# Seven half-size products in the first matmul of an attention and MLP kernel, with the LayerNorm gain folded into its weights

## Chip, cores and metric

The kernel runs on one core of a Trainium2 chip. The metric is the device time of one execution in microseconds, taken as the median of several. The kernel before took 280.4 us (median of 8 runs, 279.99 to 280.83).

## What is computed

Eight batches of 576 positions go through a linear attention with 8 heads of 64 columns, and the result x (512 columns) through LayerNorm and a two-layer MLP, with x added at the end.

```python
q_s = softmax(q over head_dim); k_s = softmax(k over positions)   # attention
kv  = einsum('bhsd,bhse->bhde', k_s, v)
x   = einsum('bhsd,bhde->bhse', q_s, kv)      # then heads side by side: 576 x 512 a batch
xn  = (x - mean) / sqrt(var + 1e-6) * g_ln
ch  = maximum(xn @ w_ch1, 0.0) @ w_ch2        # 512 -> 2048 -> 512
out = x + ch
```

## The kernel before

**Chunks.** The rows are cut into nine chunks of 512. Chunk c = 0 to 7 holds positions 0 to 511 of batch c, as 4 row groups `t` of 128; chunk 8 (`C9`) holds the last 64 positions of all eight batches. The code counts from 0 throughout, and so does this text.

**First matmul (MLP).** `xn` is transposed to `xnT`, so that its 512 columns are 4 blocks `ko` of 128 partitions. The 2048 hidden columns are 16 row tiles `m` of the transposed hidden state `hT`. `mm1` makes one row tile from 4 matmuls of 512 columns (one for each `ko`, all four row groups); `mm1_part` makes it for two row groups, with 256 columns. In chunks 2 to 8 row tiles 0 to 3 are made by `mm1_part`, 4 to 15 by `mm1`. `relu` moves each result from PSUM to `hT` on ACT (DVE takes some of chunk 0). The factor 1/std is left out of `xn` and applied at the end (`rstd_op`, `y_quarter`), since the relu commutes with a positive factor per row.

**Second matmul.** From chunk 1 on (`FAST`) it is already in Strassen's form: `mm2_fast` makes seven products of half-size blocks, 16 matmuls of 256 columns each, from `hT`, its four sums `hs` (`sum_h`, DVE) and four sums of w2 made once (`quarter_w2`). The PSUM banks are called a, b, c, e (in chunk 8 also d). Several results share products, so a bank is copied in the middle (`seed_c`, `copy_u("s2")`, `copy_u("s3")`, on ACT), products go on adding to it, and a copy is added to another bank on DVE (`seed_e`, `add_u`). Chunk 8 has its own order, `last_products`: products 1, 2, 6, 5, 7, 3, 4.

**Attention of the next chunks, as side work.** While PE works on the MLP of chunk c, the kernel also does the attention of chunk c + 1 (`attn_fast`: q reductions, `kv_mm`, evacuation to `kv_sb`, `po_mm`, `x_fast`, `xn_T`) and prepares batch c + 2 (`prep_fast`: exp of q and k on ACT, the transpose `eq_T`, the cast of v to `vm`, the remainders by `prep_kvrem`). `x_fast` scales the attention result by 1/sum of q, with the row sum as a by-product, makes the mean and calls `xn_out`, which subtracts the mean and multiplies with the broadcast gain `g_bc`. `square_sum` makes the variance on ACT.

**What sets the order.** The order on each engine is written out by hand. `run(main, side)` walks the matmuls of the chunk, each with a weight (1 for 512 columns, 0.5 for 256), and issues each piece of side work when the sum of weights reaches its number (its due time). A chunk of 512 rows has 64 + 56 = 120 units. A due time only sets the place in each engine's queue; the engines run ahead of or behind each other as their semaphores let them.

**Transfers.** SP's queue issues the loads of q, k, v and their remainders from batch 3 on, and the transposes. POOL's queue issues the weights, batches 1 and 2, and the stores of the output. v is loaded as float32 to `vt` and cast to bf16 in `vm` by ACT (batches 3 to 7), or cast by the transfer to a bf16 `vt` and copied by DVE (`CAST`: batches 1 and 2).

**PSUM.** `mm_ps` has 6 banks for the MLP, `att_ps` 2 for the attention.

Of the kernel before, what the change touches and what calls it, by code (L numbers as in the profile page):

```python
# [3 lines left out]

# [16 lines left out]
def kernel(  # L21
# [33 lines left out]
    CAST = (1, 2)  # L55
    T0 = 6
# [13 lines left out]

    ident = const.tile([P, P], BF16)
    eps_ln = const.tile([P, 1], FP32)
# [6 lines left out]
    g_bc = const.tile([P, DM], FP32)  # L79
# [22 lines left out]
    raws = {}  # L102

# [3 lines left out]
    def alloc_kv(b):  # L107
        raws[b][0], raws[b][1], raws[b][3], raws[b][4] = (
            raw.tile([P, H, T, D], FP32, tag="kt", name="kt", bufs=1),
            raw.tile([P, H, T, D], BF16 if b in CAST else FP32, tag="vt", name="vt", bufs=1),  # L110
            raw.tile([P, H // 2, D], FP32, tag="ktr", name="ktr"),
            raw.tile([P, H // 2, D], FP32, tag="vtr", name="vtr"),
        )
# [47 lines left out]
    def prep_kvrem(b):  # L161
        par = b % 2
        nc.scalar.activation(ekr[:, par], raws[b][3], AF.Exp)
        for half in range(2):
            ps = slice(SR * half, SR * half + SR)
            nc.vector.tensor_copy(
# [52 lines left out]
    def exp_k0(j):  # L219
        hs = slice(2 * j, 2 * j + 2)  # L220
        if j == 0:
            eks[0] = raw.tile([P, T0, H, D], BF16, tag="vt", name="ek0", bufs=1)
# [8 lines left out]
    def z0_mm(j):  # L231

        if j % 2 == 0:
            kvbox["z0", j // 2] = mm_ps.tile([P, 2, 256], FP32, tag="m", name="z0")
# [38 lines left out]
    def start_x(c):  # L273
# [3 lines left out]
            mlp.tile([P, T, DM], BF16, tag="xn", name="xn"),  # L277
# [6 lines left out]
    def po_mm(c, t, i):  # L284


        if c < B:
            if i == 0:
                pool, tag = (mm_ps, "m") if c == 0 and t >= 2 else (att_ps, "a")
                pobox["p"] = pobox[c, t] = pool.tile([P, DM], FP32, tag=tag, name="po")  # L290
# [22 lines left out]
    def stats(c, t, src, parts=(slice(0, 512),)):  # L313
# [3 lines left out]
        for cols in parts:  # L317
            nc.vector.scalar_tensor_tensor(
                xn[:, t, cols], in0=src[:, cols], scalar=mv[:, t, 0:1], in1=g_bc[:, cols],
# [3 lines left out]
    def square_sum(c, t):  # L323
        x, _, _, mv = xs[c]
# [4 lines left out]
    def xn_out(c, t):  # L329
        x, _, xn, mv = xs[c]  # L330
        nc.vector.scalar_tensor_tensor(  # L331
            xn[:, t], in0=x[:, t], scalar=mv[:, t, 0:1], in1=g_bc, op0=ALU.add, op1=ALU.mult
        )

    def x_fast(c, t):
# [7 lines left out]
        )  # L343
        nc.vector.tensor_scalar_mul(out=mv[:, t, 0:1], in0=st[:, t, 0:1], scalar1=-1.0 / DM)
# [15 lines left out]
    def xn_sub(c, t):  # L360
        _, _, xn, mv = xs[c]
        nc.vector.scalar_tensor_tensor(
            xn[:, t], in0=pobox[c, t], scalar=mv[:, t, 0:1], in1=g_bc, op0=ALU.add, op1=ALU.mult
# [25 lines left out]
    def rstd_op(c):  # L389
# [4 lines left out]
            lnv, mv[:, :, 1], AF.Ln, bias=eps_ln, scale=1.0 / DM  # L394
        )
        nc.scalar.activation(rstds[c], lnv, AF.Exp, scale=-0.5)
# [12 lines left out]
    def mm1(c, m, ko):  # L409
        if m == 0 and ko == 0:  # L410
            new_h()
        if ko == 0:
            hbox["ph"] = mm_ps.tile([P, T, P], FP32, tag="m", name="ph")
# [7 lines left out]
    def mm1_part(c, m, t0, tn, ko):  # L421

        if (m, t0, ko) == (0, 0, 0):
            new_h()
        half, at = divmod(t0, 2)
        if m % 2 == 0 and at == 0 and ko == 0:
            hbox["ph", m // 2] = mm_ps.tile([P, 2, 2, P], FP32, tag="m", name="ph")
# [4 lines left out]
            start=(ko == 0), stop=(ko == KO1 - 1),  # L432
# [27 lines left out]
    def mm2(c, t, ko):  # L460
        if ko == 0:
            hbox["pc"] = mm_ps.tile([P, DM], FP32, tag="m", name="pc")
# [7 lines left out]
    def mm2_stream(c, t, ko):  # L470

        if ko == 0:
            hbox["pc", t] = mm_ps.tile([P, DM], FP32, tag="m", name="pc")
# [7 lines left out]
    def quarter_w2(i, g):  # L481
# [6 lines left out]
        nc.vector.tensor_sub(out=dst, in0=x, in1=y)  # L488

# [34 lines left out]
    def bank(name):  # L524
        hbox[name] = mm_ps.tile([P, 2, DH2], FP32, tag="m", name="b" + name)
# [25 lines left out]
    def last_products(product):  # L551
# [28 lines left out]
        def seed_e():  # L580
            bank("e")
            add_u("e", "s2")

        product(1, "a", first=True, at={
            0: [lambda: sum_h(1, 0), lambda: sum_h(1, 1)],
            15: [lambda: both("a", 0, 0), lambda: sum_h(1, 2), lambda: sum_h(1, 3)]})
        product(2, "c", first=True, at={15: [lambda: both("c", 0, 0, True), lambda: store(0, 2, 0)]})
        product(6, "a", at={15: [lambda: copy_u("s2")]})
        product(5, "b", first=True)
        product(7, "a", at={1: [seed_e, lambda: both("b", 2, 1)], 15: [  # L590
# [7 lines left out]
    def mm2_fast(c):  # L598
# [33 lines left out]
        def sums(*which):  # L632
            return [lambda g=g, i=i: sum_h(g, i) for g, i in which if g or c == FAST]

        late = c == FAST
# [12 lines left out]
    def mlp_steps(c):  # L648
        full = range(KO2)
# [412 lines left out]
```

## Time and profile before

| what | value |
|---|---|
| median of 8 runs | 280.4 us |
| the profiled execution: its own time, its span | 280.14 us, 278.4 us |
| busy share of PE, DVE, ACT, POOL | 98%, 70%, 65%, 13% |
| granted clock of TensorE | 0.998 |
| chunks 2 to 6, starting at 79.74 us | 28.11, 28.10, 28.11, 28.11, 28.10 us |
| chunk 8 with the end | 30.09 us |
| first matmul, 512 columns (L414) | 368 matmuls |
| first matmul, 256 columns (L429) | 400 matmuls, 32 more of 128 columns |
| second matmul, 256 columns (L521) | 896 matmuls |

The page lists busy time by engine. A matmul's own duration is its latency, and matmuls overlap, so that the rate of a stream is read from the time of a run of them and not from the mean of one. Idle time of an engine that isn't the bound costs nothing. A bracket behind a row of the timeline gives the idle time before it and what ended it.

### The profile page before, as it was taken

To read this page: it belongs to the slowest core of one execution; us is meant where nothing else is said; L and a number is where in the kernel's file an instruction comes from. 1 tells how busy PE (TensorE), PEld (TensorE's weight loads), DVE (VectorE), ACT (ScalarE), POOL (GpSimd) and SP (SyncE) were. 2 spreads that over 40 slices of the span, in tenths; PEclk is the share of its full clock that TensorE was granted. 3 is DMA by queue.
4 is the path that set the end of the run, shared out by engine and by line. 5 is a ranking of instruction groups with operands and counts; after the bars stand their busy time and mean duration, and the time that the engine had idled before them with its cause. 6 is when DMAs were issued, how large, how long until landed. Compare 5 with 4: busy or idle time off the path is not lost.

```text
span 278.4 us, 5663 instructions
## 1 busy us (share of the span) xinstructions
PE 271.9 (98%) x2242; PEld 201.4 (72%) x2245; DVE 195.4 (70%) x457; ACT 181.8 (65%) x346; POOL 36.8 (13%) x64
## 2 busy tenths in 40 slices
PE   8999999999999999999999999999999999999994
PEld 6688855766995699558955995589659855885683
DVE  4672647988996688658865886588657929962363
ACT  4568862797887785778567866886585477526500
POOL 3832224300030003000300030003000300030000
PEclk9999999999999999999999999999999999999999
DMA  7999999899979996994599469545914410241014
GB/s 189 248 206 208 337 218 334 192 248 314 186 161 364 280 142 171 325 223 79 145 338 235 77 155 316 100 75 129 212 38 79 134 57 1 40 128 61 2 38 113
DMA packets 68844, 48.01 MB, mean 172 GB/s; under 512 B 40401, under 2 KB 65489, under 8 KB 68818
## 3 DMA queue, kind: packets, MB, share of 16 engines
q1 hardware_dynamic: 57074, 27.66, 42.7%
q0 software_dynamic: 11152, 19.47, 27.8%
q10 hardware_dynamic: 592, 0.52, 0.6%
q8 instruction: 17, 0.28, 0.4%
q14 instruction: 9, 0.07, 0.1%
HBM read 36.70 MB, written 9.44 MB: 166 GB/s over the span
## 4 chain that ended last, share of the span: by engine, by line
PE 90%; DMA 4%; DVE 3%; issue 0%; POOL 0%; DVEq 0%
PE ph L414 29%; PE ba L521 20%; PE ph L429 15%; PE bb L521 5%; PE be L521 5%; PE bc L521 5%; PE pc L474 4%; PE pkv L259 3%; DMA v<-in_v_dram 2%; PE po L291 2%; DMA qt<-in_q_dram 2%; DVE x L338 1%; PE ptr L803 1%; DVE xn L331 1%; PE po L298 1%; DVE kv_sb L268 0%
## 5 line engine op out<-in xcount | busy, mean ns | idle before, releaser
L414 PE MATMUL ph<-xnT,w_sb 128*128 128x512 bf16 x368 | 87.2, 379 | 0.0
L402 ACT ACTIVATE hT<-ph 128x512 bf16<-128x512 f32 x92 | 53.5, 598 | 18.4 <-PE ph L414 18.4
L414 PEld LDWEIGHTS <-w_sb 128*128 128x128 bf16 x368 | 34.0, 98 | 34.5 <-issue 0.2
L521 PEld LDWEIGHTS <-hs 128*128 128x128 bf16 x512 | 49.2, 98 | 5.7 <-DVE hs L505 0.2
L429 PE MATMUL ph<-xnT,w_sb 128*128 128x256 bf16 (+1 forms) x432 | 52.7, 269 | 0.0
L439 ACT ACTIVATE hT<-ph 128x512 bf16<-128x512 f32 x48 | 28.6, 600 | 24.5 <-PE ph L429 24.3
L505 DVE TENSOR_TENSOR hs<-hT 128x1024 bf16<-128x1024 bf16 x32 | 21.9, 688 | 27.8 <-ACT hT L402 27.6
L429 PEld LDWEIGHTS <-w_sb 128*128 128x128 bf16 x432 | 38.4, 98 | 4.0 <-DMA w_sb<-in_moe_w_ch_dram 0.2
L521 PEld LDWEIGHTS <-hT 128*128 128x128 bf16 x384 | 36.6, 98 | 5.2 <-ACT hT L402 0.2
L538 POOL DMA_DIRECT2D out_dram<-ot x28 | 15.0, 540 | 179.7 <-DVE ot L532 155.9
L521 PE MATMUL ba<-w_q,hs 128*128 128x256 bf16 x256 | 31.3, 273 | 0.0
L331 DVE SCALAR_TENSOR_TENSOR xn<-x,mv,g_bc 128x512 bf16<-128x512 bf16 x34 | 25.6, 752 | 1.2
L338 DVE SCALAR_TENSOR_TENSOR x<-po,rq 128x512 bf16<-128x512 f32 x30 | 20.6, 686 | 6.5 <-PE po L291 6.1
L325 ACT ACTIVATE scrap<-x,mv 128x512 bf16<-128x512 bf16 x34 | 24.6, 723 | 0.1
L291 PE MATMUL po<-kv_sb,eqT 128*128 128x128 bf16 x128 | 24.1, 219 | 0.4 <-DVE x L338 0.2
L199 DVE TENSOR_REDUCE zq<-eq 128x8 f32<-128x512 bf16 x32 | 20.1, 687 | 4.2 <-ACT eq L191 2.4
L259 PE MATMUL pkv<-vm,ek 128*128 128x129 bf16 x112 | 21.2, 220 | 0.0
L546 ACT COPY s<-ba 128x512 f32<-128x512 f32 x15 | 8.8, 585 | 16.7 <-PE ba L521 16.7
L291 PEld LDWEIGHTS <-eqT 128*128 128x128 bf16 x128 | 11.7, 98 | 7.5 <-issue 0.6
L521 PE MATMUL ba<-w_sb,hT 128*128 128x256 bf16 x128 | 16.2, 273 | 0.0
L521 PE MATMUL bb<-w_q,hs 128*128 128x256 bf16 x128 | 15.8, 273 | 0.0
L521 PE MATMUL bc<-w_sb,hT 128*128 128x256 bf16 x128 | 15.7, 272 | 0.0
(117 smaller groups left out, 337.9 us busy)
## 6 DMA issues: line engine op xcount, KB each, us to landing
out_dram<-ot POOLq DMA_DIRECT2D x32, 256.0 KB, 3.2
qt<-in_q_dram SPq DMA_DIRECT2D x5, 1024.0 KB, 7.4
kt<-in_k_dram SPq DMA_DIRECT2D x5, 1024.0 KB, 6.9
vt<-in_v_dram SPq DMA_DIRECT2D x5, 1024.0 KB, 10.7
w_sb<-in_moe_w_ch_dram POOLq DMA_DIRECT2D x8, 512.0 KB, 13.5
qt<-in_q_dram POOLq DMA_DIRECT2D x2, 1024.0 KB, 15.4
kt<-in_k_dram POOLq DMA_DIRECT2D x2, 1024.0 KB, 15.8
kt<-in_k_dram SPq DMA_DIRECT2D x4, 288.0 KB, 5.7
```

Source lines behind the costliest of these rows:

```text
L199: nc.vector.reduce_sum(eqs[c][1][:, t], eqs[c][0][:, t], axis=AX.X)
L259: nc.tensor.matmul(pkv[:, j % 2, 0:w], lhsT, rhs, start=(t == 0 and j % 2 == 0), stop=(t == last), skip_group_check=True,)
L291: nc.tensor.matmul(pobox["p"][:, i * P : i * P + P], eqTs[c][:, t, i, :], kv_sb[:, c, i, :], start=True, stop=True,)
L325: nc.scalar.activation(scrap, x[:, t], AF.Square, bias=mv[:, t, 0:1], accum_out=mv[:, t, 1:2])
L331: nc.vector.scalar_tensor_tensor(xn[:, t], in0=x[:, t], scalar=mv[:, t, 0:1], in1=g_bc, op0=ALU.add, op1=ALU.mult)
L338: nc.vector.scalar_tensor_tensor(x[:, t].rearrange("p (h d) -> p h d", h=H), in0=pobox[c, t].rearrange("p (h d) -> p h d", h=H), scalar=1. ...
L402: nc.scalar.activation(dst, src, AF.Relu)
L414: nc.tensor.matmul(hbox["ph"], w1_sb[:, ko, m * P : (m + 1) * P], xnTs[c][:, :, ko, :], start=(ko == 0), stop=(ko == KO1 - 1),)
L429: nc.tensor.matmul(ph[:, m % 2, at : at + tn], w1_sb[:, ko, m * P : (m + 1) * P], xnTs[c][:, t0 : t0 + tn, ko, :], start=(ko == 0), stop=( ...
L439: nc.scalar.activation(dst, ph, AF.Relu)
L505: nc.vector.tensor_tensor(out=dst, in0=x, in1=y, op=op)
L521: nc.tensor.matmul(hbox[bank][:, t], lhsT, rhs, start=first and (own or t == 0) and k == 0, stop=k == KH - 1, skip_group_check=True)
```

## The change

1. In chunks 2 to 8 row tiles 8 to 15 of the first matmul are made by seven products of half-size blocks (`mm1_fast`, `prod1`): the blocks are 2 of the 4 `ko`, 4 of the 8 row tiles, and 2 of the 4 row groups. They are made in two groups `g` of 2 row tiles a block. Each product is 4 matmuls of 256 columns; a group needs seven, seeds bank c from bank a on ACT, keeps bank a twice on ACT (`s2`, `s3`), seeds bank e on DVE, and ends one quarter on DVE (`last_g`) and three on ACT (`out1`). Row tiles 0 and 1 are made by `mm1_part`, 2 to 7 by `mm1`. The order is a list of tokens in `plan`, with another one, `o9`, for chunk 8. Four sums of `xnT` (`sums_x`, DVE) are needed in each chunk, and four sums of w1 once (`quarter_w1`, DVE, in chunk 1).
2. g is multiplied into w1 once (`fold_w1`, four DVE instructions in chunk 0), after a column of g is made by four small matmuls. From chunk 1 on `xn` is x minus its mean; `x_fast` writes it with a factor of 512, `xn = 512 * x - sum`, and `rstd_op` takes that out.
3. v of batches 3 to 7 is loaded by POOL in eight transfers per batch (one per head), cast on the way, into `vm`; ACT's four casts per batch go. `prep_kvrem` copies the remainder of v on ACT instead of DVE for these batches.
4. Due times are placed anew: a chunk has 60 + 56 = 116 units.
5. Memory: `ek0` takes the buffer of k instead of that of v, `g_bc` that of the new `ts` (the sums of xnT), `xn` has one buffer instead of two. `bank_of` allocates from the same 6 banks.
6. Chunk 8's second matmul: order 1, 5, 2, 6, 7, 3, 4, and bank c is seeded from bank a.

```diff
+    NG = 2
+    M0 = KO2 - 4 * NG
+    plan = dict(
+        order=('P1 0|x 0|C 0|part 0|part 2|P2 0|P5 0|x 1|P6 0|E 0|plain 3|P7 0|plain 2|P3 0|P1 1|C 1|P4 0|L 0|plain 5|P6 1|P5 1|P2 1|plain 4|E 1|P7 1|plain 6|plain 7|P4 1|L 1|P3 1').split('|'),
+        red=[9.5, 19.0, 21.0, 26.5, 35.5],
+        kv=[6.0, 26.0],
+        po=[[37.5, 42.5], [45.0, 48], [56, 67.5], [84.5, 90.0]],
+        sq=[47, 62.5, 85.0, 109.0],
+        xT=[58.0, 98.5, 110.5],
+        prep=[62, 80.0, 92.5, 95.0, 97.5, 112.5],
+        sum=60,
+        qw1=[40, 53, 59.0, 79.0],
+        o9=('x 0|x 1|P1 0|C 0|plain 3|part 0|P2 0|P6 0|plain 6|plain 4|P5 0|plain 2|plain 5|P7 0|part 2|P1 1|E 0|C 1|P4 0|L 0|P3 0|P5 1|P6 1|E 1|plain 7|P7 1|P3 1|L 1|P2 1|P4 1').split('|'),
...
     def x_fast(c, t):
...
+        if c:
+            nc.vector.tensor_scalar(
+                out=xs[c][2][:, t], in0=x[:, t], scalar1=float(DM), scalar2=st[:, t, 0:1],
+                op0=ALU.mult, op1=ALU.subtract,
+            )
+            return
         nc.vector.tensor_scalar_mul(out=mv[:, t, 0:1], in0=st[:, t, 0:1], scalar1=-1.0 / DM)
         xn_out(c, t)
...
+    def fold_w1(ko):
+        nc.vector.tensor_scalar_mul(
+            out=w1_sb[:, ko, :], in0=w1_sb[:, ko, :], scalar1=g_col[:, ko : ko + 1]
+        )
...
+    def sums_x(c, ns=range(4)):
...
+        for n in ns:
+            dst, x, y = ((t1, b12, b11), (t2, b22, t1), (t3, b22, b12), (t4, b21, t2))[n]
+            nc.vector.tensor_sub(out=dst, in0=x, in1=y)
+
+    def prod1(c, g, n, slot, i, first):
...
+        nc.tensor.matmul(hbox["q", slot][:, m], lhsT, rhs, start=first and i == 0,
+                         stop=ko == 1, skip_group_check=True)
...
+        def seed(g, src, dst):
+            hbox["q", dst] = bank_of([P, 2, 2 * P], FP32, "q", dst)
+            nc.scalar.copy(hbox["q", dst], hbox["q", src])
...
+        def seed_b(g):
+            a_, b_, c_, e_ = names(g)
+            hbox["q", e_] = bank_of([P, 2, 2 * P], FP32, "q")
+            nc.vector.tensor_tensor(out=hbox["q", e_], in0=hbox["q", b_], in1=hbox["s2", g], op=ALU.add)
+
+        def last_g(g):
+            a_, b_, c_, e_ = names(g)
+            m0 = M0 + 2 * NG + 2 * g
+            dst = hbox["h"][:, m0 : m0 + 2, 2:4].rearrange("p m t c -> p m (t c)")
+            nc.vector.tensor_tensor(out=dst, in0=hbox["q", b_], in1=hbox["s3", g], op=ALU.add)
+            nc.vector.tensor_scalar_max(dst, in0=dst, scalar1=0.0)
+
+        def keep_g(g, name):
+            hbox[name, g] = mlp.tile([P, 2, DH2], FP32, tag=name, name=name, bufs=1)
+            nc.scalar.copy(hbox[name, g], hbox["q", 10 * g])
...
+            if kind == "P1":
+                product(n, 1, a_, True)
+            elif kind == "C":
+                zero(lambda: seed(n, a_, c_))
+            elif kind == "P2":
+                product(n, 2, c_, False, [lambda: out1(n, c_, 0, 0)])
+            elif kind == "P6":
+                product(n, 6, a_, False, [lambda: keep_g(n, "s2")])
+            elif kind == "P5":
+                product(n, 5, b_, True)
+            elif kind == "E":
+                zero(lambda: seed_b(n))
+            elif kind == "P7":
+                product(n, 7, a_, False, [lambda: keep_g(n, "s3")])
+            elif kind == "L":
+                zero(lambda: last_g(n))
+            elif kind == "P3":
+                product(n, 3, e_, False, [lambda: out1(n, e_, 0, 1)])
+            elif kind == "P4":
+                product(n, 4, a_, False, [lambda: out1(n, a_, 1, 0)])
...
         product(1, "a", first=True, at={
-            0: [lambda: sum_h(1, 0), lambda: sum_h(1, 1)],
-            15: [lambda: both("a", 0, 0), lambda: sum_h(1, 2), lambda: sum_h(1, 3)]})
-        product(2, "c", first=True, at={15: [lambda: both("c", 0, 0, True), lambda: store(0, 2, 0)]})
-        product(6, "a", at={15: [lambda: copy_u("s2")]})
+            0: [lambda: sum_h(1, 0), lambda: sum_h(1, 1), lambda: sum_h(1, 2), lambda: sum_h(1, 3)],
+            15: [seed_c]})
         product(5, "b", first=True)
-        product(7, "a", at={1: [seed_e, lambda: both("b", 2, 1)], 15: [
+        product(2, "c", at={15: [lambda: both("c", 0, 0), lambda: store(0, 2, 0)]})
+        product(6, "a", at={15: [lambda: copy_u("s2"), seed_e]})
+        product(7, "a", at={0: [lambda: both("b", 2, 1)], 15: [
...
         for which in parts:
-            load_main(nc.sync, b, which, 0, H)
+            if which != 1:
+                load_main(nc.sync, b, which, 0, H)
+                continue
+            for h in range(H):
+                nc.gpsimd.dma_start(
+                    vm[:, b % 2, :, h // 2, 64 * (h % 2) : 64 * (h % 2) + 64],
+                    v[b, h, 0:SM, :].rearrange("(p t) d -> p t d", t=T),
+                )
...
+            + [(p, lambda ko=ko: fold_w1(ko)) for ko, p in enumerate((66, 69, 86, 88))]
```

In the token list `P1 0` is product 1 of group 0, `x` two of the sums of xnT, `C` the seed of bank c, `E` the seed of bank e, `L` the last sum on DVE, `part 0` and `part 2` row tiles 0 and 1 for two row groups each, `plain 3` row tile 3. In `prep` and `po` the numbers are due times: the exp of q (two halves), `eq_T`, the remainders, the exp of k (two halves); and start and end of each of the four groups of `po_mm`. The due times before were 34, 73, 77, 82, 90, 106 for `prep`, 2 to 20 for `kv`, (22, 28), (36, 43), (60, 70), (80, 92.5) for `po`, and 60, 101, 105 for `xT`.

## The prediction

> **What bounds the kernel now.** The page's first part comes first, then the head of the chain that ended last, then busy time in windows cut at the starts of the chunks (columns: length; busy of PE, weight loads, DVE, ACT, POOL with counts; clock; DMA share; GB/s), then the chain in order of time.
>
> ```profile
> PE 271.9 (98%) x2242; PEld 201.4 (72%) x2245; DVE 195.4 (70%) x457; ACT 181.8 (65%) x346; POOL 36.8 (13%) x64
> ```
> ```profile
> PE 90%; DMA 4%; DVE 3%; issue 0%; POOL 0%; DVEq 0%
> ```
> ```profile
> 0.00:51.30 51.30, 48.81 (x456) 36.03 (x460) 31.00 (x81) 30.64 (x56) 19.63 (x32) 1.00 1.13 248
> 51.30:79.74 28.44, 28.44 (x250) 22.57 (x249) 25.70 (x64) 25.43 (x49) 2.69 (x5) 1.00 0.85 218
> ...
> 135.95:164.06 28.11, 28.11 (x231) 20.82 (x229) 20.83 (x50) 20.28 (x38) 2.54 (x5) 1.00 0.80 198
> ...
> 192.17:220.27 28.10, 28.10 (x230) 20.83 (x229) 21.13 (x47) 16.44 (x33) 2.07 (x5) 1.00 0.51 113
> 220.27:248.31 28.04, 28.04 (x211) 20.18 (x209) 21.21 (x42) 16.88 (x37) 2.21 (x5) 1.00 0.21 58
> 248.31:278.40 30.09, 26.08 (x193) 18.53 (x190) 12.20 (x24) 10.14 (x17) 1.22 (x3) 0.98 0.23 70
> ```
> ```profile
> 251.81 10.36 PE ph L414 x48
> 262.17 1.75 PE ba L521 x16
> ```
>
> From 51.3 us on PE never idles. 48 matmuls of 512 columns take 10.36 us, 0.216 each; 16 of 256 take 1.75 us, 0.109 each (the 379 and 273 ns of the groups are latencies that overlap). A middle chunk is then 48 x 0.216 + 32 x 0.109 (first matmul) + 112 x 0.109 (second) + 36 attention matmuls of about 0.055 = 28.05 of its 28.11 us. The bound is the number of streamed columns; DVE (74%) and ACT (72%) hide beneath it.
>
> **The Trainium skill.** "TensorE: Matmul & The Clock Gate", Back-to-back issue gap, gives N/2.4 + 2.5 ns for an isolated matmul, 109 and 216 ns here; the trace agrees, though the same section also quotes 131 ns at N=512 in a stream, which it doesn't. "VectorE: DVE Perf Modes", The perf-mode tier table, gives bf16 tensor_scalar the 4x and tensor_tensor the 2x tier, and its walkthrough some 150 cycles fixed. The trace agrees with both tiers: a bf16 copy of 512 took 288 ns, a bf16 sum of 1024 took 688. Estimates from it: tensor_scalar of 512 0.29 us, of 2048 0.69 us; sum of 512 0.43 us. "SBUF — State Buffer", Who interferes with whom, says DVE and GpSimd share a port pair by exclusive lock; no stretch of this trace shows its price.
>
> **The change, part by part.**
>
> 1. *Products.* In the chunks c = 2 to 8 (seven), eight of sixteen row tiles cost 7 x 2 x 4 = 56 matmuls of 256 columns instead of 32 of 512 (64 halves): 8 x 0.109 = 0.87 us less per chunk. Row tiles 0 and 1 were half-size before and stay so. Weight loads (98 ns) fit under 109 ns, as the second matmul shows. Seven chunks: **-6.1 us**, if PE never waits.
>
> 2. *Work for DVE per chunk.* Added: four sums of xnT 1.7, two seeds of bank e from PSUM 2 x 0.70, two last sums with a clip 2 x (0.70 + 0.29). Removed: with g in w1, xn becomes a tensor_scalar, 0.29 for 0.752, and the 0.154 for the mean goes: 4 x -0.62; the two vr copies move to ACT, -0.57. Net +2.0, to 22.9 us of 27.2 (84%).
>
> 3. *Work for ACT per chunk.* Added: two seeds 2 x 0.57, four kept banks 4 x 0.585, two vr copies about 2 x 0.37. Removed: two relus (DVE does two of the eight quarters), -1.2, and four casts of v, 4 x -0.61. Net +0.6, to 20.9 us (77%).
>
> 4. *New waits of PE.* A result leaves PSUM about 0.20 us after PE has streamed it and the copy takes 0.58, so a product that adds to a copied bank needs 0.83 us of other work between. I walked the order of a middle chunk. P6 to P7: one full tile (0.87) and its side work for group 0, P5, P2 and a tile (1.8) for group 1. Seed c to P6: at least 0.87. P7 to P4: 1.7 both times, though the group 1 copy queues on ACT behind a square sum (0.91) and lands within 0.1 us of need. Seed e to P3: over 1.5. At the start DVE still has the old chunk's last four outputs (0.48 each, until about 1.25 us after it), then forms t1 and t2 by 2.1 us; P5 wants t1 at 2.95. Behind these DVE sums queue a q reduction and the kv evacuation, for which only po waits, over 3 us later. At the end the relus of P4 and P3 queue, done 0.15 us before row tile 14 is read. Slack is thin, not negative: I take 0.15 us of bubbles per chunk (0 to 0.5). Chunks 2 to 7: 6 x (-0.87 + 0.15) = **-4.3**.
>
> 5. *The last chunk* has nothing beside it, and its order differs. P6, then one tile (0.87), then P7, P3: e needs the kept s2 (0.83) and a DVE sum (0.70) but is read 0.87 + 0.44 after P6: 0.3 late. P3, P2 and P4 end back to back and their three relus (0.6) queue on ACT: row tile 14 is 0.4 late. DVE's sums of h for the second half come up to 0.1 late. In the second matmul the product order becomes 1, 5, 2, 6, 7: 7 adds to bank a directly after 6, whose copy s2 was hidden before by product 5:
>
> ```profile
> 265.50 1.91 PE L521 MATMUL ba<-w_q,hs 128*128 128x256 bf16 x16
> 267.24 1.91 PE L521 MATMUL bb<-w_q,hs 128*128 128x256 bf16 x16
> 267.83 0.58 ACT L546 COPY s<-ba 128x512 f32<-128x512 f32 x1 [5.03 <-PE ba L521]
> 268.99 1.91 PE L521 MATMUL ba<-w_q,hs 128*128 128x256 bf16 x16
> ```
>    Bank a rested from about 267.25 to 268.99 while bb ran; with no bb, PE waits the 0.83. Sum -0.87 + 0.8 + 0.83 = **+0.8** (-0.9 to +1.5). The tail of stores is unchanged.
>
> 6. *Start and chunk 1.* The four folds of w1 (4 x 0.69) go where DVE idled 3.2 us before v's cast and 0.95 before the q reductions: hidden; at 2x instead of 4x they'd be 2 us longer and delay kv(1) by up to 1.5. Four tiny matmuls and a copy for g's column lie where PE and DVE wait for v (until 12.97 us). The ek0 tile now holds back k of batch 1 instead of v on POOL's queue; k was issued at 14.6, after the attention matmuls that free it at 13.8, so nothing queued behind moves later. xn in 0.29 shortens chunk 1's serial chain, where PE idled 0.19 twice. In chunk 1 four sums for w1 (4 x 0.69) replace savings of as much. Together **-0.1** (-0.5 to +1.5).
>
> 7. *v by DMA.* From batch 3 POOL casts v straight into vm: eight issues per batch of 512 pieces, about 0.79 us each by the w_sb row, 6.3 us of POOL. It idles over 20 us there, its stores come 20 us later, and v is read 28 us later. SP's queue loses an issue per batch, so k's remainder, q and the transposes come up sooner. Transfer time is unknown: qr moves as many 256 B pieces and, with eqT, accounts for at most 0.51 - 0.21 = 0.30 of a chunk (8.4 us), against about 5.6 us for a plain 1 MB load: up to +0.1 on a share of 0.80. The second xnT half, issued about 4 us before the chunk's end, lands in 3.1 and is wanted 1.3 us after the start. Cost 0 (0 to +1).
>
> 8. *Side work moved.* A due time only sets the place in each engine's queue. The first exp of q goes from 34 to 62, past seven relus, two copies and a square sum, to where DVE's sums and not ACT feed PE; q is read by eqT alone. eqT goes from 77 to 92.5: on SP's queue it stays between the two xnT transposes, issues (1.9 us) some 2 us ahead of the second one's data, and its reader, po at 37.5 of the next chunk, is 12 us off. The k remainder, exp of k and vr copies end before the last kept copy is ready, about 3.3 us before the chunk's end, or up to 0.2 late; product 4, which waits for that copy, has 0.8 us of cover. kv moves from 2-20 to 6-26, so DVE's evacuation comes behind the sums of xnT; its reader po starts at 37.5, 3 us later. The four po groups keep their distance to xnT. Cost 0 (0 to +0.1 per chunk, inside the bubbles above).
>
> **Sum**: -4.3 + 0.8 - 0.1 = -3.6 us on a span of 278.4, thus 274.8; with the 1.74 around it (280.14 - 278.40) 276.5. The median of eight is 0.26 above that execution: **276.8 us**.
>
> **Rivals.**
> - *More bubbles* (the same bound, thin slack): along DVE's order the first matmul's 14.7 us hold about 13.0 of work (old outputs 1.25, sums of xnT 1.7, q reductions and reciprocal 3.0, kv 1.5, seeds 1.4, last sums 2.0, x and xn 2.1). If each link is 0.3 us longer, bubbles grow to 0.5 per chunk: 276.8 + 6 x 0.35 = 278.9. For: 84% busy, four ties above. Against: PE had no bubble at 74%.
> - *Port lock* (slower): while POOL writes v's descriptors (6.3 us at the start of chunks 2 to 5), DVE's four sums of xnT read two SBUF tensors. Were each held one issue (0.79), t1 and what follows come 3.2 late, less 0.85 slack: 2.3 us x 4 chunks = +9.3, 286.1. Break-even is 0.9 per chunk, two or three holds. Against: the page says such sums contend only with GpSimd's reads.
> - *Full gain*: no bubbles, copies in the last chunk hidden: 280.4 - 6.1 = 274.3. Against: the bank a wait.
> - *The change saves no columns' time*: half-size products at 0.125 instead of 0.109 would give it all back, 280.4. The second matmul streams such matmuls at 0.109 throughout, so I nearly exclude it.
>
> **Numbers.** A difference under 0.2% (0.56 us) can't be told from none. Forecast 0.60, full gain 0.08, more bubbles 0.18 (0.02 of it about level, 0.01 slower), port lock 0.11, no saving 0.03. Faster 0.83, same 0.05, slower 0.12. The range runs from the full gain with a little help at the start, 273.9, to bubbles of 0.6 per chunk, 279.5; the lock and about 0.07 of tails lie outside.
>
> **What would show it.** Right: chunks 2 to 7 last 27.2 to 27.5 us; 392 half-size matmuls appear for the first matmul's products; in the last chunk PE idles about 0.8 us between products 6 and 7, released by ACT's copy, and DVE's share per chunk is near 84%. Wrong: chunks over 28 us, PE waiting for DVE's sums at a chunk's start, issues of v on POOL coinciding with longer DVE sums, or xnT landing late.

## The result, and the profile after

The kernel became slower: 284.55 us median of 11 runs (280.53 to 286.97) against 280.32 us of 31 runs of the kernel before (279.74 to 280.96), ratio 1.0108 (95% interval 1.0088 to 1.0128). The forecast was 276.8 us. All ratios here leave out executions over 1.5% above the fastest of their kernel; of these 11 that is three, and the median of the other eight is 283.35 us.

The profiled execution took 286.87 us (span 285.1). It is one of the longest, since TensorE's clock dropped twice in it; so stages are compared below, and not spans; its losses in the first two stages are larger than those of a middling execution.

First the page: busy time, the granted clock in 40 slices of 7.1 us, and the head of the chain that ended last.

```profile
PE 273.5 (96%) x2362; PEld 217.4 (76%) x2365; DVE 212.9 (75%) x492; ACT 186.4 (65%) x365; POOL 67.3 (24%) x104
...
PEclk9969999999599999999999999999999999999999
```
```profile
PE 90%; DMA 4%; DVE 3%; ACT 1%; issue 0%; DVEq 0%
```

PE has 120 more matmuls and hardly more busy time. New are the two dips of the clock, in the third and the eleventh slice. The chain's head is nearly the same as before, and hides what happened: its 4% of DMA are now one wait in the middle of the kernel.

Busy time in windows cut at the chunks' starts (columns: length; busy of PE, weight loads, DVE, ACT, POOL with counts; clock; DMA share; GB/s):

```profile
0.00:54.64 54.64, 52.89 (x464) 40.21 (x468) 33.94 (x88) 30.39 (x56) 20.89 (x33) 0.94 1.11 238
54.64:90.14 35.50, 31.20 (x250) 23.55 (x249) 24.31 (x58) 24.41 (x49) 8.47 (x13) 0.90 0.92 161
90.14:117.44 27.30, 27.30 (x247) 22.37 (x245) 22.68 (x53) 21.14 (x41) 8.10 (x13) 1.00 1.21 210
...
172.03:199.32 27.29, 27.29 (x246) 22.38 (x245) 22.80 (x52) 20.64 (x40) 8.08 (x13) 1.00 0.83 146
...
226.61:253.62 27.01, 27.01 (x226) 21.91 (x225) 23.96 (x51) 18.61 (x41) 2.14 (x5) 1.00 0.23 59
253.62:285.10 31.48, 25.94 (x209) 19.90 (x206) 16.04 (x32) 12.09 (x22) 1.22 (x3) 1.00 0.22 67
```

Against the windows of the kernel before:

| stage | before | after | difference |
|---|---|---|---|
| start and chunk 0 | 51.30 | 54.64 | +3.34 |
| chunk 1 | 28.44 | 35.50 | +7.06 |
| chunks 2 to 7 | 168.57 | 163.48 | -5.09 |
| chunk 8 with the end | 30.09 | 31.48 | +1.39 |
| span | 278.4 | 285.1 | +6.7 |

The stages that the change was made for gained 5.1 us. The first two, where the forecast had next to nothing, lost 10.4.

**Chunk 1.** The chain in order of time (start, length, what) and PE's timeline around the place (the bracket is the idle time before, and what ended it):

```profile
56.61 3.30 PE ph L472 x31
59.91 12.29 DMA eqT<-eq
72.25 0.29 PE po L322
```
```profile
67.35 0.59 PE L457 MATMUL ph<-xnT,w_sb 128*128 128x512 bf16 x2
72.25 0.29 PE L322 MATMUL po<-kv_sb,eqT 128*128 128x128 bf16 x1 [4.30 <-DMA eqT<-eq]
72.33 0.63 PE L457 MATMUL ph<-xnT,w_sb 128*128 128x512 bf16 x1
```

The transpose that batch 2's attention needs landed 12.3 us after its issue (7.8 before), and PE stood for 4.30 us. Behind that a matmul of 512 columns takes 0.63 us instead of 0.38, since the granted clock had dropped (the last but two column):

```profile
68.00:72.00 4.00, 0.00 (x0) 0.00 (x0) 1.03 (x3) 0.16 (x1) 0.00 (x0) 0.86 1.47 178
72.00:76.00 4.00, 3.75 (x12) 1.61 (x13) 1.72 (x5) 1.19 (x2) 0.00 (x0) 0.50 1.04 270
76.00:80.00 4.00, 4.00 (x32) 3.19 (x31) 3.13 (x7) 1.82 (x5) 0.00 (x0) 0.79 0.00 0
```

In windows of 1 us the clock is 0.50 from about 70.9 us, while PE still waits, to 77.7: 6.8 us. What else was moving shows in the queues, first of SP and then of POOL:

```profile
57.02 0.39 SPq L146 DMA_DIRECT2D qt<-in_q_dram  x1
59.91 6.93 SPq L236 DMA_TRANSPOSE eqT<-eq  x1
```
```profile
54.71 1.86 POOL L494 DMA_DIRECT2D out_dram<-ot  x3 [1.08 <-DVE ot L488]
56.57 6.04 POOL L1168 DMA_DIRECT2D vm<-in_v_dram  x8
```

In the kernel before, SP had the same load of q ahead of the transpose, and v of batch 3 came only behind it, at 63.03 us on SP's own queue:

```profile
55.89 0.39 SPq L117 DMA_DIRECT2D qt<-in_q_dram  x1
56.57 5.74 SPq L207 DMA_TRANSPOSE eqT<-eq  x1
```

Now POOL issues the eight transfers of v of batch 3 right behind the last store, with no wait between. Their due time (40) is later than that of the transpose (14.2), but a due time holds only the queue on which something waits. All loads of `load_batch` are held by a one-element memset on DVE into their target, which DVE reaches at the due time. The changed code leaves that out for v (`which` 1):

```python
        for which in parts:
            if which != 1:
                nc.vector.memset(raws[b][which][0:1, 0, 0, 0:1], 0.0)
```

**The start.** PE's timeline of it, and the window of 13 to 21 us:

```profile
11.64 0.94 PE L1107 MATMUL gcp<-ones_f,g_row 1*128 1x1 f32 x8
12.51 0.77 PE L265 MATMUL z<-ones,ek 96*128 96x1 bf16 x24
13.15 2.72 PE L288 MATMUL pkv<-v,ek 96*128 96x128 bf16 x24
15.66 1.49 PE L903 MATMUL warm<-junk 128*128 128x256 bf16 x6
```
```profile
13.00:21.00 8.00, 7.88 (x74) 6.80 (x72) 4.23 (x12) 2.48 (x6) 3.35 (x4) 0.58 1.23 208
```

The small matmuls for g's column are four in the code; the profile shows each of these float32 matmuls as two. Behind them six `warm` matmuls take 1.49 us. The kernel before took 0.82:

```profile
13.68 0.82 PE L695 MATMUL warm<-junk 128*128 128x256 bf16 x6
```

The clock was 0.58 of full speed from 13 to 21 us. In windows of 1 us it is 0.50 from about 12.9 to 19.7: 6.8 us again.

The mean clock of the 11 executions was 0.999 (one), 0.994 (four), 0.988 (one), 0.981 or 0.982 (three) and 0.976 (two, the profiled one among them). These are nearly equal steps. Experiments 2 and 4 show single spells at half clock of 3.4 us; one costs 1.7 us of full clock, 0.6% of 283 us, which is one step, and the two spells of 6.8 us here are four steps. As an estimate from this, all but one of the 11 executions had one to four such spells; the one without took 280.53 us.

### The profile page after: what moved, and what is told of

It reads as the page before. It is cut to its first block, busy times and chain, and to the rows that moved or that the text cites. A ratio compares the mean times of both kernels' runs of the same rounds, so it can differ in the third digit from the quotient of the medians.

```text
span 285.1 us, 6073 instructions
## 1 busy us (share of the span) xinstructions
PE 273.5 (96%) x2362; PEld 217.4 (76%) x2365; DVE 212.9 (75%) x492; ACT 186.4 (65%) x365; POOL 67.3 (24%) x104
## 4 chain that ended last, share of the span: by engine, by line
PE 90%; DMA 4%; DVE 3%; ACT 1%; issue 0%; DVEq 0%
PE ba L722 19%; PE q L578 14%; PE ph L457 14%; PE ph L472 10%; PE bc L722 5%; PE be L722 5%; PE bb L722 5%; PE warm L903 4%; DMA eqT<-eq 4%; PE pc L517 4%; PE pkv L288 3%; PE po L322 3%; DVE hs L706 1%; PE ptr L1012 1%; PE po L329 1%; DVE xn L368 1%
## 5 line engine op out<-in xcount | busy, mean ns | idle before, releaser
L457 PE MATMUL ph<-xnT,w_sb 128*128 128x512 bf16 x200 | 55.1, 390 | 0.0
L447 ACT ACTIVATE hT<-ph 128x512 bf16<-128x512 f32 x50 | 29.9, 605 | 18.1 <-PE ph L457 17.5
L472 PE MATMUL ph<-xnT,w_sb 128*128 128x256 bf16 (+1 forms) x320 | 37.1, 267 | 0.1
L457 PEld LDWEIGHTS <-w_sb 128*128 128x128 bf16 x200 | 19.9, 100 | 16.6 <-issue 1.9
L1168 POOL DMA_DIRECT2D vm<-in_v_dram x40 | 29.6, 745 | 9.8 <-PE q L578 4.9
L472 PEld LDWEIGHTS <-w_sb 128*128 128x128 bf16 x320 | 29.1, 98 | 3.4 <-issue 0.2
L322 PE MATMUL po<-kv_sb,eqT 128*128 128x128 bf16 x128 | 24.9, 230 | 4.5 <-DMA eqT<-eq 4.3
L375 DVE SCALAR_TENSOR_TENSOR x<-po,rq 128x512 bf16<-128x512 f32 x30 | 20.6, 686 | 10.4 <-PE po L322 10.2
L598 ACT ACTIVATE hT<-q 128x512 bf16<-128x512 f32 x42 | 24.1, 597 | 2.8 <-PE q L578 2.6
L578 PE MATMUL q<-ts,w_q 128*128 128x256 bf16 x168 | 25.7, 273 | 0.0
L228 DVE TENSOR_REDUCE zq<-eq 128x8 f32<-128x512 bf16 x32 | 20.9, 680 | 5.9 <-ACT eq L212 3.3
L482 ACT ACTIVATE hT<-ph 128x512 bf16<-128x512 f32 x34 | 20.3, 601 | 7.3 <-PE ph L472 7.1
L578 PEld LDWEIGHTS <-w_q 128*128 128x128 bf16 x224 | 19.8, 98 | 6.1 <-issue 0.3
L650 ACT COPY s<-q 128x512 f32<-128x512 f32 x28 | 16.3, 582 | 2.5 <-PE q L578 2.4
## 6 DMA issues: line engine op xcount, KB each, us to landing
qt<-in_q_dram SPq DMA_DIRECT2D x5, 1024.0 KB, 10.8
```

The lines of the kernel that those rows point to most:

```text
L228: nc.vector.reduce_sum(eqs[c][1][:, t], eqs[c][0][:, t], axis=AX.X)
L322: nc.tensor.matmul(pobox["p"][:, i * P : i * P + P], eqTs[c][:, t, i, :], kv_sb[:, c, i, :], start=True, stop=True,)
L375: nc.vector.scalar_tensor_tensor(x[:, t].rearrange("p (h d) -> p h d", h=H), in0=pobox[c, t].rearrange("p (h d) -> p h d", h=H), scalar=1. ...
L447: nc.scalar.activation(dst, src, AF.Relu)
L457: nc.tensor.matmul(hbox["ph"], w1_sb[:, ko, m * P : (m + 1) * P], xnTs[c][:, :, ko, :], start=(ko == 0), stop=(ko == KO1 - 1),)
L472: nc.tensor.matmul(ph[:, m % 2, at : at + tn], w1_sb[:, ko, m * P : (m + 1) * P], xnTs[c][:, t0 : t0 + tn, ko, :], start=(m % 2 == 0 and a ...
```

## The experiments

**1. Hold v (gate_v).** The memset is made for v too, into `vm`.

```diff
-            if which != 1:
-                nc.vector.memset(raws[b][which][0:1, 0, 0, 0:1], 0.0)
+            cell = vm[0:1, b % 2, 0, 0, 0:1] if which == 1 else raws[b][which][0:1, 0, 0, 0:1]
+            nc.vector.memset(cell, 0.0)
```

> The changed kernel, but POOL's transfers of v into vm wait again for a one-element DVE memset at the load's due time, as the loads of k and q do. Theory (without that memset POOL runs ahead and issues batch 3's eight v transfers at 56.6 us, into the q load and the transpose eqT of batch 2, which lands 12.3 us after its issue instead of 7.8): PE's idle 4.3 us before po in chunk 1 falls below 1 us, the halved clock behind it goes, chunk 1 comes back from 35.5 us to 28.2 to 29.5, and the time falls by 4 to 7 us, to about 279 to 280, since the slower start stays. Rival (eqT is late because the start is 3.3 us late and q's load with it): eqT still lands over 10 us after its issue, chunk 1 stays over 33 us, the time about 283.

278.3 us (276.73 to 279.12), ratio 0.9923 (0.9897 to 0.995). The wait put back is worth 6.25 us by the medians, 5.2 by the ratios, and turns slower into faster. POOL's line:

```profile
62.10 6.04 POOL L1168 DMA_DIRECT2D vm<-in_v_dram  x8 [7.85 <-PE pkv L288]
```

v now goes out at 62.1 instead of 56.6 us. (The bracket names a matmul of PE, but releasers are inferred; DVE's memset into `vm` ended at 61.52 us.) The transpose, issued at 56.73, landed after 6.5 us, PE didn't wait for it, and chunk 1 was back at 28.4 us. The start still varies: two of the six executions kept a clock of 0.998 and took 276.73 (the profiled one) and 276.83 us, the other four had 0.990 to 0.992 and took 277.57 to 279.12.

**2. g's column by a transfer (g_by_dma), and both (gate_and_dma).** The eight small matmuls go.

```diff
+        nc.sync.dma_start(g_col, bass.AP(moe_g_ln.tensor, moe_g_ln.offset, [[1, P], [P, KO1]]))
...
-        gcp = bank_of([P, KO1], FP32, "gcp")
-        for ko in range(KO1):
-            nc.tensor.matmul(
-                gcp[:, ko : ko + 1], g_row[:, ko * P : ko * P + P], ones_f[:, 0:1], start=True, stop=True
-            )
-        nc.vector.tensor_copy(out=g_col, in_=gcp)
```

> The changed kernel, but the column of g is loaded by a small transfer on SP's queue; the eight one-column matmuls, their bank and the DVE copy are gone. Theory (these matmuls keep the array nearly empty for 0.8 us and what follows finds the clock granted at half, 0.58 over 13 to 21 us): the clock stays near 1.0 over 13 to 21 us, the first row tile of chunk 0 starts at 17 to 17.5 us instead of 20.8, and the time falls by about 3.5 us; the wait for eqT in chunk 1 stays in part. Rival (the dip has another origin): the clock still dips in some runs and the time stays spread over several us.

> Both edits together. Theory (the two places are all that separates the result from the forecast): chunks 2 to 7 as in the changed kernel (27.3 us), start and chunk 1 within 0.5 us of the kernel before, 275.8 to 277.0 us, with a spread of under 1 us. Rival (a third loss at the start or in chunk 1): over 278.

g_by_dma: 283.75 us (283.16 to 284.1), ratio 1.0115 (1.01 to 1.0129); gate_and_dma: 276.83 us (276.63 to 277.92), ratio 0.9878 (0.9863 to 0.9894). Alone, g_by_dma gained 0.8 us by the medians (284.55 to 283.75) and nothing by the ratios, where 3.5 were expected: the 3.34 us lost at the start of the profiled execution were taken for those of a middling one. The pair with and without the small matmuls (278.3 and 276.83) puts 1.5 us on them, the pair with and without the hold (283.75 and 276.83) 6.9 us on v. With both gone the time is the forecast's. In the profiled execution of g_by_dma the start ran at full clock, and chunk 1 shows its loss alone, PE's line first, then the windows around it:

```profile
69.61 0.23 PE L322 MATMUL po<-kv_sb,eqT 128*128 128x128 bf16 x1 [4.65 <-DMA eqT<-eq]
```
```profile
64.00:72.00 8.00, 3.35 (x18) 1.49 (x17) 2.46 (x8) 2.06 (x6) 0.00 (x0) 0.90 1.54 223
72.00:76.00 4.00, 4.00 (x30) 2.83 (x29) 3.17 (x7) 1.76 (x5) 0.00 (x0) 0.78 0.32 41
```

In windows of 1 us the clock is 0.50 from about 70.3 to 73.8: one spell of 3.4 us, which began 0.7 us behind the wait.

**3. The small matmuls in the kernel before (before_gcp), and at another place (gcp_late).** before_gcp adds them to the kernel before, behind the copy of g's broadcast. gcp_late is gate_v with them moved into chunk 0's stream:

```diff
+            + [(50, make_g_col)]
```

> The kernel before, with only the small matmuls for g's column and their copy added behind the copy of g's broadcast (the column is not used). Theory A (these 0.9 us of nearly empty matmuls let TensorE's clock drop in some executions): the fastest executions stay near 280.2, others rise to 282 to 284 with a mean clock below 0.99, and the median goes up by 0.3 to 2 us. Theory B (the drop belongs to something else that the change brings to the start): 280.4, within 0.6 us, clock 0.998 in all.

> The changed kernel with v of batch 3 held by a memset as the other loads are, and the small matmuls for g's column at due time 50 of chunk 0, in the middle of a dense stream, instead of at the start. Theory A (what counts is the place, where PE has little other work): no executions with a lower clock at 13 to 21 us; 276.8 plus at most 0.9 for the matmuls in PE's stream, thus 276.8 to 277.8, spread under 1.4 us. Theory B (the matmuls lower the clock wherever they lie): a drop near 38 us instead, 278.3 or more, spread 2.4 us as with the memset alone.

before_gcp: 281.51 us median of 21 (280.06 to 283.59), ratio 1.0041 (1.0022 to 1.0059). Its executions fall in two groups: ten at a mean clock of 0.998 or more took 280.06 to 280.93 us, eleven at 0.988 to 0.994 took 281.51 to 283.59. Of the kernel before, run alongside, one of 43 was below 0.997 (0.994, at 281.76 us). The one trace of before_gcp is of an execution without a drop, so that the drops of the eleven lie at the start is inferred from the edit. gcp_late: 277.6 us, all four between 277.46 and 277.75, ratio 0.9903 (0.989 to 0.9916), clock 0.998 to 1.0. So theory A holds for both: at the start these matmuls bring drops of the clock in about half of the executions; in a dense stream they cost about 0.8 us (277.6 - 276.83), near the 0.94 us that they take, and in these four executions no clock.

**4. Half of v early (half_early), and half of each piece early (thin_early).** Both build on g_by_dma. In the first, four of batch 3's eight transfers run ahead and four are held. In the second, eight transfers of 32 of the 64 columns run ahead and eight of the other 32 are held.

```diff
+                if b == 3 and h == 4:
+                    nc.vector.memset(vm[0:1, b % 2, 0, 2, 0:1], 0.0)
```
```diff
+            for d0 in ((0, 32) if b == 3 else (0,)):
+                dn = 32 if b == 3 else 64
+                if d0:
+                    nc.vector.memset(vm[0:1, b % 2, 0, 0, 32:33], 0.0)
...
-                    vm[:, b % 2, :, h // 2, 64 * (h % 2) : 64 * (h % 2) + 64],
-                    v[b, h, 0:SM, :].rearrange("(p t) d -> p t d", t=T),
+                        vm[:, b % 2, :, h // 2, 64 * (h % 2) + d0 : 64 * (h % 2) + d0 + dn],
+                        v[b, h, 0:SM, d0 : d0 + dn].rearrange("(p t) d -> p t d", t=T),
```

> The changed kernel with g's column loaded by a small transfer, and of batch 3's eight transfers of v the first four free to run ahead as in the changed kernel, the last four held by a memset until the due time. Theory A (v's bytes and pieces share the DMA engines with the transpose eqT, so its delay grows with their number): eqT lands about 9.5 us after its issue, between 6.4 (all held) and 12.6 (none held); PE waits about 1.5 us for it instead of 4.65; 278.3 to 279.5. Theory B (any such transfer ahead of the transpose holds it up, by its place in a queue): eqT still lands at 12 us or later, 283.2 to 284.1. Theory C (the last ones collide alone): 276.8.

> The changed kernel with g's column loaded by a small transfer; v of batch 3 in two halves by columns: eight transfers of 32 of the 64 columns run ahead, eight of the other 32 are held by a memset until the due time. The early part has as many pieces as all of v, and half its bytes. Theory A (the number of pieces counts): eqT lands 11.5 us or more after its issue, nearly as with all of v early (12.6); PE waits 3.5 us or more, 282 to 284. Theory B (the bytes count): as with half of the heads early, eqT 9.8 us, PE waits 1.9, 278.5 to 280.

half_early: 279.53 us (277.42 to 282.94), ratio 0.9953 (0.9934 to 0.9972); eqT landed in 9.8 us:

```profile
68.03 0.23 PE L322 MATMUL po<-kv_sb,eqT 128*128 128x128 bf16 x1 [1.86 <-DMA eqT<-eq]
```

Landing at 6.4 us with none early, 9.8 with half, 12.6 with all: in these traces, one each, the delay grows with how much of v goes ahead (theory A). Its profile also shows a drop of the clock at the start, to 0.79 in the window of 13 to 21 us (0.50 from about 14.0 to 17.4), with no small matmul for g in the kernel. There PE waited 0.69 us for v of batch 0 behind the one-column `z` matmuls:

```profile
13.52 0.69 PE L288 MATMUL pkv<-v,ek 96*128 96x128 bf16 x9 [0.69 <-DMA v<-in_v_dram]
```

So in this execution it wasn't g's matmuls: a thin stretch of another kind stood before the drop. It doesn't always do so: waits of 0.44 and 0.45 us at the same place (q_late and fill_idle) left the clock at 1.00. Nine of the 22 executions, this one among them, had a mean clock of 0.992 to 0.994; where it dropped in the other eight isn't known.

thin_early: 281.94 us (278.64 to 284.93), ratio 1.0021 (0.9996 to 1.0046). In its profile eqT landed in 10.8 us and PE waited 2.79, between the two theories, which wanted 11.5 or 9.8. But that execution, of 279.79 us, is one of the three fastest of 14; the other eleven took 281.34 us or more, and the median is just short of the 282 to 284 of theory A. Also only seven of the eight early transfers went out at once (the last at 62.1 us), so whether pieces or bytes count stays open.

**5. Fill the wait (fill_idle).** g_by_dma with 40 matmuls on constant data in place of PE's wait; they write into the bank that the attention matmul then overwrites.

```diff
+            if (c, t, i) == (2, 0, 0):
+                for _ in range(40):
+                    nc.tensor.matmul(pobox["p"][:, 0:256], junk[:, 0:P], junk[:, 0:256], start=True, stop=True)
```

> The changed kernel with g's column loaded by a small transfer, and 40 matmuls of 256 columns on constant data put on PE directly before the attention matmul that waits for eqT (their result is overwritten by it); v of batch 3 stays free to run ahead. They take 40 x 0.109 = 4.4 us of the 4.65 us wait. Theory A (the half clock after the wait comes of PE's idling): PE idles 0.3 us, the clock stays 1.0 in 68 to 76 us, and what is left of the loss is the wait: 283.75 - 2.3 = 281.5. Theory B (the clock drops for another reason): the clock near 70 to 76 us stays at about 0.5 to 0.8, and 283.7.

282.2 us (280.72 to 283.03), ratio 1.0063 (1.0042 to 1.0084), against 1.0115 for g_by_dma. The windows around the place:

```profile
64.00:72.00 8.00, 8.00 (x69) 5.98 (x67) 2.90 (x9) 2.84 (x7) 0.00 (x0) 1.00 1.49 229
72.00:76.00 4.00, 4.00 (x42) 3.63 (x40) 3.96 (x9) 3.11 (x8) 0.00 (x0) 1.00 0.12 17
```

The transpose was nearly as late (11.6 us, against 12.6 in g_by_dma), PE went on with the attention matmuls at 69.37 us (69.61), and the clock stayed at 1.00; in all six executions its mean was 0.996 or more, where the four of g_by_dma had 0.988 to 0.994. Theory A: the half clock is a consequence of PE's idling, and costs about 1.5 us (283.75 - 282.2; 2.3 expected) on top of the wait.

**6. q behind the transpose (q_late).** g_by_dma, v free to run ahead, but q of batch 3 due at 20 instead of 8.

```diff
-        s += [(p, lambda w=w: load_batch(3, (w,))) for p, w in ((8, 2), (31, 0), (40, 1))]
+        s += [(p, lambda w=w: load_batch(3, (w,))) for p, w in ((20, 2), (31, 0), (40, 1))]
```

> The changed kernel with g's column loaded by a small transfer, v of batch 3 free to run ahead, and the load of q of batch 3 moved behind the transpose eqT on SP's queue (due time 20 instead of 8). Theory A (v's transfers alone hold the transpose up): eqT still lands 10.5 us or more after its issue, PE waits 2.5 us or more, 281 to 283.5. Theory B (it takes both, v and q, ahead of the transpose): eqT lands within 8 us, no wait, 276.8 to 277.3.

277.36 us (277.29 to 277.51), ratio 0.9889 (0.9876 to 0.9902). SP's queue, POOL's, and the landing of eqT:

```profile
57.65 3.36 SPq L236 DMA_TRANSPOSE eqT<-eq  x1
61.12 0.51 SPq L146 DMA_DIRECT2D qt<-in_q_dram  x1
```
```profile
55.72 6.09 POOL L1163 DMA_DIRECT2D vm<-in_v_dram  x8
```
```profile
DMA to landing us min/median/max: 7.3/7.3/7.3
```

v still went out at 55.7 us, and eqT landed in 7.3 us: theory B, against what I had thought likelier. v alone ahead does no harm, q alone ahead doesn't either (the kernel before: 7.8 us; gate_v: 6.5). It takes both. Whether it matters that v is cast on the way, or moves in small pieces, wasn't tried.

**7. Without the products (products_off).** gate_and_dma with row tiles 2 to 15 made by 512-column matmuls in chunks 2 to 8, without sums of xnT.

```diff
-        order=('P1 0|x 0|C 0|part 0|part 2|P2 0|P5 0|x 1|...
+        order=['part 0', 'part 2'] + ['plain %d' % m for m in range(2, 16)],
...
-        o9=('x 0|x 1|P1 0|C 0|plain 3|part 0|P2 0|P6 0|...
+        o9=None,
```

> The changed kernel with v held by a memset and g's column by a small transfer, but without the seven products: row tiles 2 to 15 are made by matmuls of 512 columns in chunks 2 to 8, without the sums of xnT; all other parts of the change stay. Theory A (the gain is the products' columns): chunks 2 to 7 go back to 28.1 us, the first matmul of chunk 8 loses its stalls; 276.8 + 6 x 0.81 + about 0.2 = 281.9 (281.0 to 282.6). Theory B (the other parts bring some of the gain, by less work on DVE and ACT): 279 or less.

284.36 us (283.66 to 284.75), ratio 1.0134 (1.0117 to 1.0152): 7.5 us above gate_and_dma, 5.1 expected. PE's waits in it (what waited, for what, us in total, times, longest):

```profile
PE bb L722 <- DVE hs L706: 1.2, 4, 0.3
...
PE ba L722 <- ACT s L748: 0.7, 1, 0.7
PE ph L472 <- DMA xnT<-xn: 0.6, 1, 0.6
```

The columns explain 7 x 0.87 = 6.1 us. Four waits for sums of h (1.2) and one for xnT (0.6) are new; that they come of side work whose places are made for the other order is likely, not tested. Against them, chunk 8 is rid of its stalls in the first matmul. The direction of theory A holds; the other parts, placed as they are, gain nothing without the products. My expectation left out the waits, and took too little for chunk 8.

**8. Chunk 8 (gate_dma_last, hs_first).** The first is gate_and_dma with product 2 behind product 6, so that it runs while bank a is copied. The second also puts two sums of h that are read late behind four that are read soon.

```diff
-        product(2, "c", at={15: [lambda: both("c", 0, 0), lambda: store(0, 2, 0)]})
         product(6, "a", at={15: [lambda: copy_u("s2"), seed_e]})
+        product(2, "c", at={15: [lambda: both("c", 0, 0), lambda: store(0, 2, 0)]})
```
```diff
-        s9=[54.5, 58.0, 58.0, 58.5],
+        s9=[54.5, 58.0, 60.5, 60.5],
```

> Both edits, and in chunk 8 the products of the second matmul in the order 1, 5, 6, 2, 7, 3, 4, so that product 2 runs while bank a is copied. Theory: PE's 0.68 us of idle time before product 7 goes, 0.6 to 0.9 us less than with both edits alone, about 275.5. Rival: product 6 comes earlier and waits for DVE's sums instead; no gain.

> The changed kernel with v held by a memset, g's column by a small transfer, chunk 8's second matmul in the order 1, 5, 6, 2, 7, 3, 4, and two sums of h of the first half, which only products 7 and 3 read, put behind the four of the second half on DVE. Theory A (product 5 waits 0.34 us for the first of those four): that wait goes, 276.38 - 0.34 = 276.0. Theory B (another wait takes its place, for the sums put back): 276.4.

gate_dma_last: 276.38 us (276.12 to 276.84), ratio 0.9856 (0.9843 to 0.9869). hs_first: 275.36 us (275.17 to 275.76), ratio 0.9819 (0.9806 to 0.9831), the fastest version here, 1.8% below the kernel before. gate_dma_last gained 0.45 us on gate_and_dma (0.6 to 0.9 expected), and PE no longer waits ahead of product 7. PE's timeline of products 5, 6, 2 and 7 in gate_dma_last, and then of 5, 6 and 2 in hs_first:

```profile
258.85 0.60 PE L722 MATMUL bb<-w_q,hs 128*128 128x256 bf16 x4
259.79 1.48 PE L722 MATMUL bb<-w_q,hs 128*128 128x256 bf16 x12 [0.34 <-DVE hs L706]
261.12 1.91 PE L722 MATMUL ba<-w_q,hs 128*128 128x256 bf16 x16
262.86 1.91 PE L722 MATMUL bc<-w_sb,hT 128*128 128x256 bf16 x16
264.61 1.91 PE L722 MATMUL ba<-w_q,hs 128*128 128x256 bf16 x16
```
```profile
258.67 1.91 PE L722 MATMUL bb<-w_q,hs 128*128 128x256 bf16 x16
260.41 1.91 PE L722 MATMUL ba<-w_q,hs 128*128 128x256 bf16 x16
262.16 1.91 PE L722 MATMUL bc<-w_sb,hT 128*128 128x256 bf16 x16
```

Product 5 begins 2.27 us ahead of product 6 in the first and 1.74 in the second: the bracket of 0.34 was worth 0.53, since a bracket leaves out the gap that the modelled ends of the last matmuls cover. The rest of the 1.0 us between the medians isn't explained by this place.

## Why the prediction was wrong

**Step 7 (v by DMA, cost 0, range 0 to +1) failed**, and with it the sign. It asked when v is read and whether POOL has time, and found slack in both. It didn't ask what holds v back: the memset was the due time, and the diff made it conditional. Nor did it ask whose transfers v would meet: it says that the transposes "come up sooner", when the one in chunk 1 landed 4.5 us later. Its reasoning for the later chunks is right, since none of them shows a wait; batch 3, loaded in chunk 1, is the one that it didn't walk through. The measured term is +5.2 to +6.9 us, by the pair of kernels and by whether medians or ratios are compared: 4.3 to 4.65 of waiting in the two traces that show it, about 1.5 of half clock (experiment 5), and a remainder.

The Trainium skill has both links of that chain. "DMA: Bandwidth & Descriptors", Queues, rings and completion order, says that each DMA engine serves the queues that have work in turn, packet by packet. That fits experiment 6: q and eqT are on SP's queue, v on POOL's; with q first, q gets through more slowly beside v (9.1 us to landing against 6.6 before), and eqT stands behind it. That this is the mechanism is argued; the runs show that it takes both loads, and that the delay grows with v's amount. "TensorE: Matmul & The Clock Gate", What's actually happening, says that a window of about 3.4 us without activity halves the clock, and that the window doesn't begin with the kernel. The traces agree: in the wait of 4.30 us the clock fell to 0.50 after some 2.9 us, and 0.7 us behind the wait of 4.65 us in g_by_dma; waits of 1.86 us (half_early) and 2.79 us (thin_early) left it at 1.00; and with the wait filled it stayed at 1.00.

**Step 6 (start, -0.1, range -0.5 to +1.5) failed in one sentence.** It put g's matmuls where "PE and DVE wait for v" and costed them at nothing. Their time is indeed hidden: the two executions of gate_v at a clock of 0.998 took 276.73 and 276.83 us, as without them (276.83). What it left out is the clock, which in other executions dropped behind them. The profiled execution lost 3.34 us there; by the medians it is 0.8 to 1.5 us, inside the range or at its edge. The same page speaks of idling; the profiled execution shows no idle time of PE in that stretch, only 1.7 us of one-column matmuls, and that was enough in about half of the executions of before_gcp. How thin a stretch must be, and for how long, the runs don't settle.

**Steps 1, 2, 3 and 4 held.** Chunks 2 to 7 were forecast at -4.3 us and gave -5.09: of 6 x 0.87 = 5.22 only 0.02 per chunk was lost, where 0.15 was allowed for bubbles. PE is busy throughout. In chunks 3 and 4 DVE took 22.7 us (forecast 22.9) and ACT 20.6 (20.9). The subtraction that makes xn took 0.35 us, not the estimated 0.29. The port lock didn't come: the sums of xnT took 0.36 to 0.43 us each in chunks 2 to 7, near the estimate of 0.43; the last two of each of chunks 2 to 5 ran while POOL issued v (in chunk 2 at 92.38 and 92.71 us, POOL from 92.02 to 94.99) and took 0.41 to 0.42.

**Step 5 (chunk 8, +0.8) held within its range.** The chunk grew by 1.39 us, PE's part of it by 1.0. Of its stalls, product 7 starts 2.59 us after product 6 (1.75 without a stall), so 0.84 was lost for the copy, forecast 0.83; the bracket reads 0.68:

```profile
272.74 1.91 PE L722 MATMUL ba<-w_q,hs 128*128 128x256 bf16 x16
275.33 1.91 PE L722 MATMUL ba<-w_q,hs 128*128 128x256 bf16 x16 [0.68 <-ACT s L748]
```
```profile
274.69 0.58 ACT L748 COPY s<-ba 128x512 f32<-128x512 f32 x1 [5.14 <-PE ba L722]
```

The copy began 0.20 us after PE had streamed product 6 (274.49 to 274.69), as step 4 has it. In the lines of the kernel before that the prediction shows it began 0.58 us after (267.25 to 267.83), which is left unexplained there and here.

The same reading of PE's starts gives 0.27 for product 3's row tiles (forecast 0.3), 0.21 at the start of product 1 (0.4), and 0.51 for the sums of h at product 5 (at most 0.1: too small). The tail of stores, taken as unchanged, grew by 0.37.

With both faults mended the sum of the prediction is met, 276.83 us measured and 276.8 forecast, but that is partly luck. By stages the trace of gate_and_dma stands against the kernel before at +0.19 us at the start, +0.01 in chunk 1, -5.09 in chunks 2 to 7 and +1.39 in chunk 8; the forecast had -0.1 for the first two, -4.3 and +0.8. The errors cancel.

**Step 8** cost nothing that shows: PE doesn't wait in chunks 2 to 7.

## What to carry to other kernels

When a load moves to another queue, look for what held it back in the old one (here a one-element write into its target), and list which transfers it will now meet, above all a transpose that has little slack. Work for TensorE that is put into a waiting stretch isn't free if it streams next to nothing; put it into a dense stream, or do it with a small transfer. And price a long wait of TensorE with the slower clock behind it (here waits of 4.30 and 4.65 us had it, waits of 1.86 and 2.79 didn't).

## What the runs showed of the hardware

- A wait of TensorE of 4.30 us came with 6.8 us at half clock, one of 4.65 us with 3.4 us; waits of 1.86 and 2.79 us left the clock at 1.00. Matmuls on constant data in place of the wait kept it at 1.00 and saved about 1.5 us.
- The spells at half clock in three traces lasted 3.4 us (g_by_dma, half_early) or 6.8 us (both in the changed kernel), and the mean clocks of the changed kernel's executions lie in steps of 0.006, one spell of 3.4 us each.
- Eight one-column float32 matmuls (0.94 us) ahead of 24 one-column bf16 ones (0.75 us) went with a lower clock in 11 of 21 executions of the kernel before, at a cost of 1 to 3 us each time; without the eight it was one of 43.
- A transpose of a 128 x 2048 bf16 tile landed in 6.4 to 7.8 us with either 1 MB of q or v's transfers ahead of it, and in 11.6 to 12.6 with both.
